# Block-sparse attention and a gated feed-forward: the values' product in column halves, and a hand-set order of all steps

## The chip, the cores and the metric

The kernel runs on one core of a Trainium2 chip. The metric is the device time of one execution in microseconds, as a median over runs. The engines are TensorE (PE; its weight loads are listed apart as PEld), VectorE (DVE), ScalarE (ACT), GpSimd (POOL) and SyncE (SP), which issues most of the DMAs. TensorE writes its results into PSUM; DVE and ACT read them there.

## What is computed

Four batches of eight heads, 768 tokens, 64 columns a head. A token is in one of 24 blocks of 32. A query block sees its neighbours, the first and the last block, and three blocks drawn per query block; the first and the last query block see everything. The attention's result, 512 columns a token, goes through a gated feed-forward layer.

```python
scores = scale * np.matmul(q, k.transpose(0, 1, 3, 2))
...
scores = np.where(mask, scores, -1000000000.0)
scores = scores - np.max(scores, axis=-1, keepdims=True)
attn = np.exp(scores)
attn = attn / (np.sum(attn, axis=-1, keepdims=True) + 1e-09)
return np.matmul(attn, v).astype(np.float32)
...
x = np.ascontiguousarray(attn_out.transpose(0, 2, 1, 3)).reshape(B * S, H * D)
g = x @ w_gate
silu = g * (1.0 / (1.0 + np.exp(-g)))
val = x @ w_val
return (silu * val @ w_out).astype(np.float32)
```

## The kernel before

**Tiles and chunks.** The queries of a batch are 6 tiles of 128 (four blocks each). `CHUNKS` (L29) groups the tiles: batch 0 in three chunks of two, batches 1 to 3 in two chunks of three each, so chunks 3 to 8 hold batches 1 to 3. A chunk goes through attention (`attention`, L1051), then through the feed-forward layer (`ffn_in`, L1611, and `ffn_out`, L1736). Batches 1 to 3 have 22 sparse query blocks each (66 in all): 12 in the first chunk, 10 in the second, whose last tile holds two sparse blocks and the two that see everything.

**Numbers in two parts.** In batches 1 to 3 and in the feed-forward of chunks 2 to 8, a float32 number is held as two float16 numbers, a high part and a low part that is the rest. A product of two such numbers is three float16 products: high by high, high by low, low by high.

**A sparse block of batches 1 to 3** (`block`, L1098). Its keys are copied together into one of three slots (`kring`, by DVE, L1112 to L1115), its values into one of three slots (`vring`: the neighbours by a DMA of SP, L1121, the drawn blocks by an indirect DMA of POOL, L1124). In the order of the steps:
- `scores` (L1131): 32 matmuls (two blocks, eight heads, two parts of the queries) make one step of PE; each uses 32 of the array's columns (four at a time, `tile_position`), into PSUM tile `qk`.
- `top` (DVE, L1151), `power` (ACT, L1168), `inv` (DVE), `high` (ACT, L391) and `low` (DVE, L394): mask and maximum, exponential and sum, reciprocal, weights in two parts into `pp`.
- `turn` (L1193): a DMA transpose on SP's queue into `pts`, of which there are three.
- `product` (L1195): weights times values on PE into PSUM tile `pv`, which two blocks share. For each pair of heads j, over two halves cc of the 256 keys, and over three combinations of parts, one matmul has both heads' values as stationary weights (128 columns) and both heads' attention weights as moving columns (64). The result has 128 rows and 64 columns; only the two quarters in which the head of the values is the head of the weights are used.
- `x_high` (ACT, L1227) and `x_low` (DVE, L1232), once for two blocks: the used quarters go as high and low part into the chunk's input `xall` of the feed-forward, in two operations of 64 partitions each.

The blocks that see everything (`full_rows`, L886) have their own steps. There the scores (L922) and the product (L991) already use 64 columns of the array a matmul, and the product already has the weights' high and low parts side by side: a matmul with the values' high part moves 128 columns, one with the low part 64, and `gather` (L1005) adds the two halves.

**Feed-forward.** For each of 12 groups of 128 hidden columns, `ffn_in` multiplies twice (12 matmuls each, L1693; L1687 in chunks 0 and 1), then ACT and DVE form the gated product, which ACT (`high`, L1712) and POOL (`low`, L1715) split into `h`. `ffn_out` multiplies by the second weight in steps of 9 matmuls (L1756) and stores.

**What sets the order.** All steps are tasks of `Plan` (L120). A task has an engine, a cost in us written beside it, the tasks that it needs, buffers that it takes from rings, and a rank. `order` (L164) plays the program through with these costs: whenever an engine is free, the ready task with the lowest rank (then the earliest number) goes next, if its buffers are free; a task that needs another is ready 0.16 us (`SEM_US`) after the other's end. The order found is the order of the instructions on each engine, and it is fixed when the program is built. Ranks come from the loops (attention of chunk ci at 10 ci, its feed-forward 1000 higher) and a table `SHIFT` (L47) with one number for each key, which several tasks share (a block's whole sequence, for one).

Of the kernel before, what the change touches and what calls it, by code (L numbers as in the profile page):

```python
# [13 lines left out]
ALU = mybir.AluOpType  # L14
# [4 lines left out]
BLK = 32  # L19
# [22 lines left out]
DMA_US = 1.6  # L42
SEM_US = 0.16
# [3 lines left out]
SHIFT = {  # L47
# [54 lines left out]
}  # L102


class Task:
# [122 lines left out]
def tile_block_sparse_attn_swiglu(  # L228
# [1580 lines left out]
    for t in plan.order():  # L1809
        t.emit()  # L1810
# [44 lines left out]
```

## Time and profile before

| | us |
|---|---|
| median of 3 runs | 801.23 (798.42, 801.23, 802.46) |
| profiled execution | 800.0 |
| its span, first to last instruction | 798.2 |
| PE busy | 762.4 |
| DVE busy | 547.4 |
| ACT busy | 504.5 |
| POOL busy | 205.7 |
| mean granted TensorE clock | 0.989 of full speed |

The span is what the profile covers; the execution's time has 1.8 us around it. Busy times count an engine's own instructions, not its waits or the issue of DMAs. PE's matmuls overlap each other, so a matmul's duration (0.19 us for one of 64 columns) is much longer than the step from one start to the next; what a piece of work costs PE is read from its first start to the start of the piece behind it. In a timeline, adjacent instructions of one line are merged and their number stands behind an x.

### The profile page before, as it was taken

Reading aid. Unit: us, or ns where it says so; the run is one execution under the profiler, and the core shown is the slowest. Engines: PE = TensorE matmul, PEld = TensorE weight load, DVE = VectorE, ACT = ScalarE, POOL = GpSimd, SP = SyncE. Lnnn points to the kernel's source line nnn. Section 1 sums busy time; section 2 is a strip of 40 time slices with the busy share of each in tenths; the row PEclk is TensorE's granted clock in tenths of the full one; section 3 lists DMA queues with packets and bytes.
Section 4 is the critical chain, followed back from the end, with each engine's and each line's share of the span. In section 5 each row is a group of like instructions: output and inputs, shape, how many; then the busy total and the mean of one; then the engine's idle time right before and its main releaser. Section 6 shows DMA issues by size and latency. Waiting matters only on the chain.

```text
span 798.2 us, 21196 instructions
## 1 busy us (share of the span) xinstructions
PE 762.4 (96%) x8098; PEld 489.2 (61%) x8098; DVE 547.4 (69%) x1658; ACT 504.5 (63%) x1211; POOL 205.7 (26%) x257
## 2 busy tenths in 40 slices
PE   3789999999999999999999999999999999999998
PEld 2557778884587566645665566645665566555655
DVE  5676898998898787742799866753798767731220
ACT  2687767587688686763598856754487757641221
POOL 3553511322033223201223222401223233101210
PEclk9889999999999999999999999999999999999999
DMA  8963537647877979478769994947878974330001
GB/s 205 259 220 118 193 146 260 205 125 230 198 151 172 212 169 197 91 197 265 159 134 182 269 227 114 203 97 211 188 133 179 228 177 105 69 69 19 1 1 39
DMA packets 171430, 128.08 MB, mean 160 GB/s; under 512 B 115008, under 2 KB 136896, under 8 KB 171328
## 3 DMA queue, kind: packets, MB, share of 16 engines
q1 hardware_dynamic: 165696, 109.42, 56.6%
q0 software_dynamic: 5632, 17.31, 8.5%
q8 instruction: 63, 1.03, 0.5%
q14 instruction: 39, 0.32, 0.1%
HBM read 79.50 MB, written 11.01 MB: 113 GB/s over the span
## 4 chain that ended last, share of the span: by engine, by line
PE 63%; DVE 18%; DMA 8%; issue 4%; ACT 4%; SPq 1%; DVEq 1%; ACTq 0%
PE p L1693 29%; PE po L1756 18%; PE pv L1206 4%; PE p L1687 3%; DMA q<-in_q_dram 3%; PE qk L1137 3%; DVE pp L394 2%; DVE act L1702 1%; DVE act L1707 1%; DMA pts<-pp 1%; DVE w1t L394 1%; DVE e L1151 1%; DMA stage<-in_k_dram 1%; DVE kring L1114 1%; PE qk L1341 1%
## 5 line engine op out<-in xcount | busy, mean ns | idle before, releaser
L1693 PE MATMUL p<-xall,w1t 128*128 128x384 f16 (+1 forms) x2016 | 326.8, 319 | 0.0
L1693 PEld LDWEIGHTS <-w1t 128*128 128x128 f16 x2016 | 191.2, 98 | 115.5 <-issue 8.5
L1715 POOL TENSOR_TENSOR h<-act,h 128x384 f16<-128x384 f32 (+1 forms) x108 | 101.6, 941 | 372.5 <-ACT h L1712 372.1
L1756 PE MATMUL po<-w2all,h 128*128 128x512 f16 (+1 forms) x900 | 195.3, 371 | 0.3 <-DVE w2all L394 0.3
L1756 PEld LDWEIGHTS <-h 128*128 128x128 f16 x900 | 84.6, 98 | 93.7 <-issue 5.6
L1712 ACT CAST h<-act 128x384 f16<-128x384 f32 (+1 forms) x108 | 50.8, 471 | 82.5 <-DVE act L1707 82.2
L1124 POOL DMA_INDIRECT w2all<-vd,vidx x66 | 62.8, 951 | 150.2 <-PE pv L1206 126.7
L1702 DVE SCALAR_TENSOR_TENSOR act<-act,p 128x384 f32<-128x384 f32 (+1 forms) x108 | 54.2, 504 | 65.2 <-ACT act L1698 64.5
L1687 PE MATMUL p<-xall,w1t 128*128 128x256 f32 x384 | 88.8, 384 | 0.4 <-DVE act L1702 0.3
L1168 ACT ACTIVATE e<-e,nb,es 128x256 f32<-128x256 f32 x132 | 78.2, 593 | 2.2
L1687 PEld LDWEIGHTS p<-xall,w1t 128*128 128x128 f32 x384 | 71.4, 192 | 12.0 <-DVE w2all L394 1.4
L1698 ACT ACTIVATE act<-p,gsc 128x384 f32<-128x384 f32 (+1 forms) x84 | 47.0, 560 | 31.2 <-PE p L1693 30.6
L1707 DVE SCALAR_TENSOR_TENSOR act<-act,hs,p 128x384 f32<-128x384 f32 (+1 forms) x84 | 49.7, 591 | 21.8 <-PE p L1693 18.8
L1206 PEld LDWEIGHTS <-w2all 128*128 128x128 f16 x1584 | 55.1, 98 | 13.9 <-issue 3.8
L394 DVE SCALAR_TENSOR_TENSOR pp<-e,rr,pp 128x256 f16<-128x256 f32 x132 | 61.2, 510 | 1.3 <-ACT pp L391 1.0
L391 ACT ACTIVATE pp<-e,rr 128x256 f16<-128x256 f32 x132 | 58.1, 496 | 3.7 <-DVE rr L782 2.5
L1206 PE MATMUL pv<-pts,w2all 128*128 128x64 f16 x1584 | 57.0, 193 | 2.8 <-DMA pts<-pp 2.8
L1151 DVE CUSTOM_DVE_ANT_1 e<-qk,msk 128x256 f32<-128x256 f32 x132 | 50.0, 417 | 2.8 <-issue 2.4
L1593 ACT ACTIVATE ot<-po,oc 128x512 f32<-128x512 f32 (+1 forms) x25 | 16.7, 667 | 42.9 <-PE po L1756 42.7
L1114 DVE COPY kring<-kst 128x256 f16 x198 | 38.9, 251 | 5.6 <-PE qk L1137 5.3
L1232 DVE TENSOR_TENSOR xall<-pv,xall 64x256 f16<-64x256 f32 x66 | 27.7, 420 | 21.1 <-ACT xall L1227 18.7
L1137 PE MATMUL qk<-kring,qs 128*32 128x256 f16 x1056 | 35.7, 274 | 0.2 <-DVE mx L1151 0.2
(187 smaller groups left out, 899.4 us busy)
## 6 DMA issues: line engine op xcount, KB each, us to landing
stage<-in_w_dram SPq DMA_DIRECT2D x36, 512.0 KB
w2all<-vd SPq DMA_DIRECT2D x66, 192.0 KB
qs<-qraw SPq DMA_DIRECT2D x72, 128.0 KB
out_dram<-ot SPq DMA_DIRECT2D x19, 256.0 KB
qn<-in_q_dram SPq DMA_DIRECT2D x36, 128.0 KB
qraw<-in_q_dram SPq DMA_DIRECT2D x36, 128.0 KB
stage<-in_v_dram SPq DMA_DIRECT2D x9, 512.0 KB
vd<-stage SPq DMA_DIRECT2D x9, 512.0 KB
```

The lines of the kernel that those rows point to most:

```text
L391: nc.scalar.activation(hi, src, AF.Copy, scale=scale)
L394: nc.vector.scalar_tensor_tensor(lo, src, scale, hi, op0=ALU.mult, op1=ALU.subtract)
L1124: nc.gpsimd.indirect_dma_start(vf[0:96, 1, :], None, bt.vd, bass.IndirectOffsetOnAxis(ap=vidx[0:96, qb : qb + 1], axis=0))
L1137: nc.tensor.matmul(stv[u * BLK : (u + 1) * BLK, g].rearrange("p s k -> p (s k)"), o.q[:, l, h // 2, h % 2, col : col + BLK], kg[:, h].rear ...
L1151: nc.vector.tensor_tensor_reduce(ev[:, g], stv[:, g], o.g.msk[:, qb, :].unsqueeze(2).broadcast_to([P, 8, BLK]), scale=1.0, scalar=-3.0e38, ...
L1168: nc.scalar.activation(ev[:, g], ev[:, g], AF.Exp, bias=nb_[:, g : g + 1], scale=o.g.es[:, 0:1], accum_out=c["rs"][:, g : g + 1],)
L1206: nc.tensor.matmul(pvv[:, j, n % 2], vg[:, cc, l, 2 * j : 2 * j + 2, :], pq[:, g, m, cc, u : u + 2, :], start=i == 0, stop=i == 5,)
L1687: nc.tensor.matmul(t[:, 0:tc_], w[:, i + 1, k_ * P : (k_ + 1) * P], x_k(k_), start=k_ == 0, stop=k_ == NKT - 1)
L1693: nc.tensor.matmul(t[:, 0:tc_], w_[:, f, m, k_, :], x_k(k_, l), start=i == 0, stop=i == 11)
L1702: nc.vector.scalar_tensor_tensor(a_, a_, 1.0, pg.tile[:, 0:tc_], op0=ALU.add, op1=ALU.mult)
L1715: nc.gpsimd.tensor_tensor(hv(f)[:, 1, :], act.tile[:, 0:tc_], hv(f)[:, 0, :], op=ALU.subtract)
L1756: nc.tensor.matmul(po.tile[:, cs], hv(f)[:, l, ts_], w2h[:, f, m, cs], start=f == 0 and i == 0, stop=f == NF - 1 and i == 2)
```

## The change

Four things, in one diff.

1. `product` of sparse blocks in batches 1 to 3 gives each head its own matmul with 64 stationary columns, in the lower or upper half of the array's columns (`hh`), as `full_rows` has it. The weights' high and low parts lie side by side as moving columns: 64 with the values' high part, 32 (the high part alone) with the low part. 32 matmuls a block in place of 24. `pv` keeps its shape; all of it is used now, as two halves that have to be added.
2. `x_high` copies the first half, rounded to float16, for all 128 partitions at once. `x_low` subtracts that from the first half and then adds the second half.
3. The planner knows column-tiled steps (`thin`): scores and products of batches 1 to 3. Going into or out of a column-tiled stretch costs 0.097 us in its model (`TURN_US`). In such a stretch, a ready column-tiled step goes before any other. A product with `thin=2`, which all have but those of a chunk's last tile, may start outside such a stretch only 4 us (`HOLD_US`) after it is ready. Between two steps of PE the model has no 0.16 us any more. Some costs are changed.
4. `SHIFT` is gone; every task gets a rank of its own from a list, `RANKS`, in the order in which the tasks are made.

```diff
+TURN_US = 0.097
+HOLD_US = 4
...
-SHIFT = {
...
-}
+RANKS = [
+    2700.7, 4581.1, 52.9, 1659, 2895.2, 1629.7, 100.2, 120.7, 2159.2, 8107.9, 4611.5, 731.4, 5241.2, 5293.2, 1337.4,
...
+]
...
-        t.rank = rank + SHIFT.get(t.key, 0.0)
+        t.rank = rank
...
-                    if t.ready > now:
-                        later.append(t.ready)
+                    at = t.ready + (HOLD_US if t.thin == 2 and not thin else 0.0)
+                    if at > now:
+                        later.append(at)
                         continue
-                    if best is not None and (t.rank, t.no) > (best.rank, best.no):
+                    key = (eng == "PE" and thin and not t.thin, t.rank, t.no)
+                    if best is not None and key > low:
                         continue
...
+                us = t.us
+                if eng == "PE":
+                    us += TURN_US if bool(t.thin) != thin else 0.0
+                    thin = bool(t.thin)
...
-                    x.ready = max(x.ready, t.end + SEM_US if x in t.outs else free[eng])
+                    x.ready = max(x.ready, free[eng] if x not in t.outs or eng == x.eng == "PE" else t.end + SEM_US)
...
-            s = in_turn("qk", "PE", 0.87, scores, [o.done] + bt.k_done, rank, take=qk, use=[o.qs, bt.ks])
+            s = in_turn("qk", "PE", 0.66, scores, [o.done] + bt.k_done, rank, take=qk, use=[o.qs, bt.ks], thin=True)
...
-            pvs.append(in_turn("pv", "PE", 0.68, product, there + vl, rank, take=[] if j else [pv],
-                               use=turned + vbuf + ([pv] if j else [])))
+            pvs.append(in_turn("pv", "PE", 0.54, product, there + vl, rank, take=[] if j else [pv],
+                               use=turned + vbuf + ([pv] if j else []), thin=True))
...
-                a = in_turn("qk", "PE", 1.0, lambda first=first: [x[1]() for x in first], [x[0] for x in first] + [o.done], r,
-                            take=qks, use=[o.qs])
+                a = in_turn("qk", "PE", 0.87, lambda first=first: [x[1]() for x in first], [x[0] for x in first] + [o.done], r,
+                            take=qks, use=[o.qs], thin=True)
...
-            pvv = pv.tile.rearrange("p (j b q) -> p j b q", j=4, b=2)
+            out_ = pv.tile.rearrange("p (j b lq) -> p j b lq", j=4, b=2)
 
             for j in range(4):
-                g, u = divmod(2 * j, 4)
-                i = 0
                 for cc in range(2):
-                    for l, m in ((0, 0), (0, 1), (1, 0)):
-                        nc.tensor.matmul(
-                            pvv[:, j, n % 2],
-                            vg[:, cc, l, 2 * j : 2 * j + 2, :],
-                            pq[:, g, m, cc, u : u + 2, :],
-                            start=i == 0,
-                            stop=i == 5,
-                        )
-                        i += 1
+                    for l, w in ((0, 2), (1, 1)):
+                        for hh in range(2):
+                            g, u = divmod(2 * j + hh, 4)
+                            nc.tensor.matmul(
+                                out_[hh * D : (hh + 1) * D, j, n % 2, 0 : w * BLK],
+                                vg[:, cc, l, 2 * j + hh, :],
+                                pq[:, g, 0:w, cc, u, :],
+                                start=cc == 0 and l == 0,
+                                stop=cc == 1 and l == 1,
+                            )
...
         def x_high():
-            for hh in range(2):
-                src, hi, _ = x_views(hh)
-                nc.scalar.copy(hi, src)
+            src, _, hi, _ = x_views()
+            nc.scalar.copy(hi, src)
 
         def x_low():
-            for hh in range(2):
-                src, hi, lo = x_views(hh)
-                nc.vector.tensor_tensor(lo, src, hi, op=ALU.subtract)
+            src, more, hi, lo = x_views()
+            nc.vector.tensor_tensor(lo, src, hi, op=ALU.subtract)
+            nc.vector.tensor_tensor(lo, more, lo, op=ALU.add)
...
-        a = in_turn("pv", "PE", 0.71, product, [a, vl, vi], rank, take=[pv] if n % 2 == 0 else [], use=[pts] + ([pv] if n % 2 else []))
+        a = in_turn("pv", "PE", 0.47, product, [a, vl, vi], rank, take=[pv] if n % 2 == 0 else [], use=[pts] + ([pv] if n % 2 else []), thin=1 if last else 2)
...
-            a = add("ACT", 0.76, x_high, [a, x_open(ci, rank)], rank, use=[pv, xts[ci]])
-            x_done[ci].append(add("DVE", 0.87, x_low, [a], rank, use=[pv, xts[ci]]))
+            a = add("ACT", 0.42, x_high, [a, x_open(ci, rank)], rank, use=[pv, xts[ci]])
+            x_done[ci].append(add("DVE", 0.88, x_low, [a], rank, use=[pv, xts[ci]]))
...
+    for t, rank in zip(plan.tasks, RANKS, strict=True):
+        t.rank = rank
```

The feed-forward's `high` copies also get a dependence on the first copy into the same `h` buffer, in the planner's order alone.

More of the change, by code (lines that the diff above doesn't have):

```diff
@@ L42 @@
 DMA_US = 1.6
+TURN_US = 0.097
+HOLD_US = 4
 SEM_US = 0.16
 LANES = 8
-SHIFT = {
[54 rows of a table removed]
-}
+RANKS = [
[183 rows of a table added]
+]
 class Task:
-    __slots__ = ("eng", "us", "emit", "need", "rank", "take", "dma", "left", "outs", "next", "ready", "end", "no", "key", "late", "many")
+    __slots__ = ("eng", "us", "emit", "need", "rank", "take", "dma", "left", "outs", "next", "ready", "end", "no", "key", "late", "many", "thin")
 class Buf:
@@ L128, in ring, with add @@
         self.depth[name], self.given[name] = n, []
-    def add(self, eng, us, emit, need=(), rank=0.0, take=(), use=(), dma=None, behind=None, late=0.0, many=1):
+    def add(self, eng, us, emit, need=(), rank=0.0, take=(), use=(), dma=None, behind=None, late=0.0, many=1, thin=False):
         t = Task()
+        t.thin = thin
         t.late, t.many = late, many if dma is not None and eng != "POOL" else 0
@@ L174, in order @@
         done = []
+        thin = False
         now = 0.0
@@ L197, in order @@
                         continue
-                    best = t
+                    best, low = t, key
                 if best is None:
@@ L204, in order @@
                     self.given[b.ring].append(b)
-                free[eng] = now + t.us
-                t.end = now + t.us + t.late
+                us = t.us
+                if eng == "PE":
+                    us += TURN_US if bool(t.thin) != thin else 0.0
+                    thin = bool(t.thin)
+                free[eng] = now + us
+                t.end = now + us + t.late
                 if t.dma is not None:
-                    queue = max(max(queue, now + min(0.4, t.us)) + t.dma, t.end)
+                    queue = max(max(queue, now + min(0.4, us)) + t.dma, t.end)
                     t.end = queue + DMA_US
@@ L1087, in attention @@
                 pv = Buf("pv")
-                two = [block(ci, b, bt, o, sub, n + i, sparse[n + i], qbs.index(sparse[n + i]) * BLK, r + 0.05 * i, tsc, pv)
+                two = [block(ci, b, bt, o, sub, n + i, sparse[n + i], qbs.index(sparse[n + i]) * BLK, r + 0.05 * i, tsc, pv,
+                             sub == len(CHUNKS[ci]) - 1)
                        for i in range(2)]
@@ L1096, in attention, with block @@
                         pass
-    def block(ci, b, bt, o, sub, n, qb, col, rank, tsc, pv):
+    def block(ci, b, bt, o, sub, n, qb, col, rank, tsc, pv, last):
         nq = f"{b}_{qb}"
@@ L1215, in block, with x_views @@
         cols = slice(sub * P + col - BLK, sub * P + col + BLK)
-        def x_views(hh):
-            hs_ = slice(hh * D, (hh + 1) * D)
-            pvv = pv.tile.rearrange("p (j b q) -> p j b q", j=4, b=2)
-            src = pvv[hs_, :, :, hh * BLK : (hh + 1) * BLK]
+        def x_views():
+            pvv = pv.tile.rearrange("p (j b l q) -> p j b l q", j=4, b=2, l=2)
             xt = xts[ci].tile
-            return [src] + [xt[hs_, l, :, cols].rearrange("p j (b q) -> p j b q", b=2) for l in range(2)]
+            return [pvv[:, :, :, i, :] for i in range(2)] + [xt[:, l, :, cols].rearrange("p j (b q) -> p j b q", b=2) for l in range(2)]
@@ L1246, in block @@
         a = add("SP", 1.3, turn, [a], rank, take=[pts], use=[pp], dma=1.5)
-        a = in_turn("pv", "PE", 0.71, product, [a, vl, vi], rank, take=[pv] if n % 2 == 0 else [], use=[pts] + ([pv] if n % 2 else []))
+        plan.key = f"c{ci}.{sub}.{n}"
+        a = in_turn("pv", "PE", 0.47, product, [a, vl, vi], rank, take=[pv] if n % 2 == 0 else [], use=[pts] + ([pv] if n % 2 else []), thin=1 if last else 2)
+        plan.key = f"b{ci}.{sub}.{n}"
         v_read[slot] = [a]
         if n % 2 == 1:
-            a = add("ACT", 0.76, x_high, [a, x_open(ci, rank)], rank, use=[pv, xts[ci]])
-            x_done[ci].append(add("DVE", 0.87, x_low, [a], rank, use=[pv, xts[ci]]))
+            a = add("ACT", 0.42, x_high, [a, x_open(ci, rank)], rank, use=[pv, xts[ci]])
+            x_done[ci].append(add("DVE", 0.88, x_low, [a], rank, use=[pv, xts[ci]]))
     def open_q0(ci, rank):
@@ L1729, in ffn_in @@
             new = f % many == 0
-            a = add("ACT", s_[4], high, [a], EVAC, take=[hb] if new else [], use=[act] + ([] if new else [hb]))
+            a = add("ACT", s_[4], high, [a], EVAC, take=[hb] if new else [], use=[act] + ([] if new else [hb]),
+                    behind=None if new else first_h)
+            first_h = a if new else first_h
             h_done.append(add("POOL", s_[5], low, [a], EVAC, use=[act, hb]))
```

236 rows, old and new, of tables (RANKS, SHIFT) are left out of this document.

## The prediction

> **What bounds the kernel now.** I read the page's busy times first, then the chain that ended last, then the busy time by stage, then TensorE's own timeline.
>
> ```profile
> span 798.2 us, 21196 instructions
> PE 762.4 (96%) x8098; PEld 489.2 (61%) x8098; DVE 547.4 (69%) x1658; ACT 504.5 (63%) x1211; POOL 205.7 (26%) x257
> ...
> PE 63%; DVE 18%; DMA 8%; issue 4%; ACT 4%; SPq 1%; DVEq 1%; ACTq 0%
> ```
>
> TensorE (PE) is busy nearly throughout, and the chain runs mostly over it. The stages say where:
>
> ```profile
> 0.00:50.00 50.00, 29.88 (x656) 21.30 (x660) 32.15 (x97) 27.85 (x72) 21.67 (x46) 0.86 0.92 241
> 50.00:150.00 100.00, 95.35 (x1348) 76.03 (x1331) 84.04 (x184) 70.33 (x178) 33.32 (x51) 0.98 0.54 181
> 150.00:725.00 575.00, 567.18 (x5685) 349.91 (x5684) 417.18 (x1354) 390.30 (x935) 139.70 (x149) 1.00 0.73 168
> 725.00:798.20 73.20, 70.00 (x431) 41.95 (x429) 14.04 (x24) 16.01 (x29) 10.96 (x12) 1.00 0.05 15
> ```
>
> The columns are the stretch and its length, then PE, PEld, DVE, ACT and POOL busy with their instruction counts, the granted clock, DMA share and GB/s. From 150 us on PE stands idle 7.8 us before 725 and 3.2 us after, at full clock. So in the stage where the change works, PE time taken away is time gained, as long as PE is still fed. Batch 0 and its loads (first 150 us) hold the other 24.8 us of idle; the new product does not touch them.
>
> How far PE stays fed is read from the end. The chain's last long pieces, and the last attention result:
>
> ```profile
> 724.80 46.80 PE p L1693 x288
> 771.60 23.41 PE po L1756 x144
> ```
>
> ```profile
> L1232 DVE TENSOR_TENSOR xall<-pv,xall x66: 404/422/428, 237.9 to 713.7; 64x256 f16<-64x256 f32 x66
> ```
>
> The last chunk's feed-forward takes 46.80 + 23.41 = 70.2 us, and 3.2 us follow it. It needs all of that chunk's attention, which is finished at 713.7 + 0.4 = 714.1. PE comes to it at 724.8, so attention has 10.7 us in hand.
>
> **The product, piece by piece.** Now each sparse block has 24 matmuls with whole-array weights and 64 moving columns, of which half the output (one head's weights against the other head's values) is thrown away. The columns below are start, duration, engine and what ran:
>
> ```profile
> 308.92 0.86 PE L1206 MATMUL pv<-pts,w2all 128*128 128x64 f16 x24
> 309.62 2.11 PE L1693 MATMUL p<-xall,w1t 128*128 128x384 f16 x12
> 311.57 0.86 PE L1206 MATMUL pv<-pts,w2all 128*128 128x64 f16 x24
> ...
> 314.22 0.86 PE L1206 MATMUL pv<-pts,w2all 128*128 128x64 f16 x24
> ...
> 317.74 4.07 PE L1693 MATMUL p<-xall,w1t 128*128 128x384 f16 x24
> 321.74 0.71 PE L991 MATMUL pvf<-ptsf,stage 128*64 128x128 f16 x24
> 322.38 2.12 PE L1693 MATMUL p<-xall,w1t 128*128 128x384 f16 x12
> 324.44 0.84 PE L922 MATMUL qkf<-kst,qs 128*64 128x384 f16 x8
> ...
> 329.97 1.06 PE L1137 MATMUL qk<-kring,qs 128*32 128x256 f16 x32
> 330.96 2.12 PE L1693 MATMUL p<-xall,w1t 128*128 128x384 f16 x12
> ```
>
> From 308.92 to 309.62 a product holds PE for 0.70 us: 0.70 / 24 = 29 ns a matmul. The new one has 32 matmuls with 64 weight columns, in 16 pairs whose halves lie in different column halves of the array: 8 pairs with 64 moving columns, 8 with 32. The kernel has such pairs already, in the full rows' product (L991), 12 of them, half with 128 and half with 64 columns:
>
> ```profile
> L991 PE MATMUL pvf<-ptsf,stage 128*64 128x128 f16 x144 | 8.2, 226 | 0.0
> L991 PE MATMUL pvf<-ptsf,stage 128*64 128x64 f16 x144 | 7.6, 193 | 0.0
> L1206 PE MATMUL pv<-pts,w2all 128*128 128x64 f16 x1584 | 57.0, 193 | 2.8 <-DMA pts<-pp 2.8
> ```
>
> That piece lasts 0.71 to the end of its last matmul, which takes 0.19 (the 193 ns row), so its 24 matmuls start within 0.52 us: 11 steps of about 47 ns between 12 pairs, the first step slower. If the halves did not run together, 12 matmuls of 64 columns at 29 ns and 12 of 128 at about twice that would take over 1 us. So the halves do run together, and a pair costs about what one whole-array matmul of the same width costs. For the 64-wide pair I take 29 ns. For the 32-wide pair no row has a price; halving gives 15 ns, the 29 ns row is the other end if a step has a floor. I take 29, the nearest row. Then a product is 16 x 0.029 = 0.47 us (0.35 with 15 ns), and 66 blocks (1584 / 24) save 66 x 0.23 = **15.4 us** (23.1 at the other end).
>
> **The turns.** Before a whole-array product an FFN group of 12 takes 311.57 - 309.62 = 1.95. Before a column-tiled piece it takes 324.44 - 322.38 = 2.06, so entering costs 0.10. Leaving: the scores (L1137) hold PE for 330.96 - 329.97 = 0.99. They are 8 steps of four tiles, 256 columns each; at the whole-array rate (1.95 / 12 for 384 columns, so 0.108 for 256) that is 0.87, so 0.12 goes on the first step and on leaving. A group of column-tiled pieces costs **0.22 us** on top of its work. Today the products pay none of it, and the other column-tiled pieces stand alone:
>
> ```profile
> L1137 PE MATMUL qk<-kring,qs 128*32 128x256 f16 x1056 | 35.7, 274 | 0.2 <-DVE mx L1151 0.2
> L922 PE MATMUL qkf<-kst,qs 128*64 128x384 f16 x96 | 10.3, 332 | 0.5 <-ACT ef L944 0.3
> ```
>
> 1056 / 32 = 33 pieces of scores, 96 / 8 = 12 of full-row scores and 288 / 24 = 12 full-row products make 57 groups. The planner now lets a product of a chunk's first tiles wait up to 4 us for company (48 of the 66; the last tiles' 18, which are 4 and 2 in each of three batches, don't wait), and in a column-tiled stretch it picks such pieces first. Products come 2.65 us apart above (308.92, 311.57, 314.22), so a wait of 4 us catches the next one as a rule. My estimate is that the 66 products add 28 groups to the 57, after counting those where scores or full rows share one. Bounds: a few fewer than 57 when nearly every product rides with scores, and 57 + 66 when none does. 28 x 0.22 = **6.2 us lost**.
>
> A group that mixes 32-column scores with 64-column products turns inside as well, if a change of width is a turn; no row has the two side by side. I take nothing for it, and up to 0.22 for each in the range. [...]
>
> **Emptying the products.**
>
> ```profile
> L1232 DVE TENSOR_TENSOR xall<-pv,xall 64x256 f16<-64x256 f32 x66 | 27.7, 420 | 21.1 <-ACT xall L1227 18.7 <-ACT h L1712 1.2 <-issue 0.5
> L1227 ACT CAST xall<-pv 64x256 f16<-64x256 f32 x66 | 24.0, 363 | 18.1 <-PE pv L1206 17.5
> L1469 DVE TENSOR_TENSOR xall<-pv,xall 128x256 f16<-128x256 f32 x3 | 1.2, 414 | 0.0
> L1468 ACT CAST xall<-pv 128x256 f16<-128x256 f32 x3 | 1.1, 370 | 0.0
> ```
>
> ACT does one copy over 128 partitions (0.37) in place of two over 64 (0.73): 33 x 0.36 = 11.9 us of ACT time less, all of it beside PE. DVE still does two operations, at 0.41 in place of 0.42, one of them now an addition of the second half. Neither is on the path; nothing goes into the sum. Its cover is the 10.7 us in hand; were that gone, ACT's part would be a gain.
>
> **A rank per step.** All steps get a new place, on every queue, SP's loads and transposes and POOL's gathers included; PE's steps that follow PE's are modelled without a semaphore's delay. None of that adds an instruction. What it can win is bounded by the idle time: 7.8 us in 150 to 725 and 24.8 before, much of the latter first loads. One stall of the kind that an order can remove:
>
> ```profile
> 350.22 0.16 PE L388 MATMUL nrm_v<-vacc,ones_h 128*128 128x3 bf16 x1 [1.28 <-ACT stage L398]
> ```
>
> I take **3 us gained**, between 8 lost (the idle of 150 to 725 doubled) and 8 gained. The wait added to the products has this queued behind it, off PE:
>
> ```profile
> POOL w2all L1124 <- PE pv L1206: 126.7, 51, 22.1
> ```
>
> The gather of the next values waits for a product to free one of three slots, as the transposes on SP wait for one of three transposed weights. A held product passes its delay on to both. I price that at nothing while the 10.7 us last.
>
> **The sum**: -15.4 + 6.2 - 3 = -12.2 us on the profiled execution's 800.0, so 787.8. The median of the runs shown, 801.2, lies 1.2 above it; on that scale the forecast is **789 us**.
>
> **The rivals.** *Attention sets the end* (17%): if attention still ends at 714.1, the rest is 70.2 + 3.2, a span of 787.5, or 789.3 with the 1.8 around it (800.0 against 798.2) and 790.5 on the median's scale. For it: the slots of three and the single end point; against it: ACT is relieved and the order is free to bring attention forward.
>
> *More than forecast* (13%): 32-wide pairs at 15 ns save 23.1, with 4 us of turns, 3 of idle gained and an earlier end of attention: 801.2 - 22 = 779. It needs attention about 11 us earlier, which speaks against it.
>
> *The change does not group* (13%): the waits seldom find company, 66 new groups cost 14.5 against 15.4 saved, and nothing else is gained: 800. For it are the 18 products that don't wait and stretches in which a product finds no other piece within its wait; against it is the 2.65 us spacing.
>
> *Weight loads set the pace* (5%), slower than before: 16 pairs now bring 16 double loads in 0.47 us, and the densest such stretch seen is this:
>
> ```profile
> 321.74 0.58 PEld L991 LDWEIGHTS <-stage 128*64 128x64 f16 x24 [0.32 <-issue]
> ```
>
> Its 12 pairs of loads, each about 0.11 long, start within 0.47 us, 43 ns a pair. [...] If 43 ns is the loads' own pace, a product takes 16 x 0.043 = 0.69, nothing is saved, and the turns stay: 801.2 + 6.2 = 807. It decides from 44 ns a pair on, where the saving is gone. [...]
>
> *The holds starve PE* (7%), slower too: 8 held products in a chunk go through three slots, 2.7 rounds, at up to 4 us each 10.7 us in a chunk, 21 in the last batch's two. Attention then ends at 735 and the time is 801.2 - 10.7 + 21 = 812. It decides where the holds' delay in the last batch passes 10.7 us.
>
> **How the numbers follow.** My forecast's own case has 45%. A difference of 0.5%, 4 us, is about what a measurement of this kernel can tell from none. Faster than 797 are the forecast, attention's end and the larger gain: 0.75. Within 0.5% is the change that does not group: 0.13. The two slow rivals make 0.12. The range goes from the larger gain, 778, to just over the ungrouped case, 802, and leaves the slow rivals and the best edge out.
>
> **What would show it.** Right: products of 0.46 to 0.49 us from start to start inside a group, pair steps of 28 to 30 ns, 75 to 95 column-tiled groups after 200 us, ACT's busy time down by about 12 us, PE idle in the middle stage still below 10 us, and the last attention result near 705 to 712. Wrong: pair steps over 40 ns (weight loads), 110 groups or more (no grouping), or new PE gaps that end on DMA of the transposes or on gathers, with the last feed-forward starting as soon as the last attention result is there (attention or holds).

## The result, and the profile after

The changed kernel takes 808.6 us (median of 7 runs, 805.4 to 810.3) against 801.1 for the kernel before (7 runs, 798.4 to 810.2): a ratio of **1.0081, 95% interval 1.0052 to 1.0111**. 789 was forecast, with 802 as the upper end. Here and below, a ratio leaves out runs more than 1.5% above the fastest run of their kernel, which are one of before's and four of the twelve of e11_pairs_slot. The profiled execution took 810.32 us, its span is 808.5.

Busy times of the changed kernel:

```profile
span 808.5 us, 22153 instructions
PE 761.2 (94%) x8626; PEld 484.3 (60%) x8626; DVE 548.1 (68%) x1658; ACT 491.5 (61%) x1178; POOL 206.6 (26%) x257
```

PE did not become less busy (762.4 before), though the product is less work, and the span grew by 10.3. By stage, columns as in the prediction:

```profile
50.00:150.00 100.00, 95.47 (x1398) 77.33 (x1397) 86.97 (x191) 74.11 (x188) 37.31 (x53) 0.97 0.57 192
150.00:725.00 575.00, 556.11 (x6165) 339.25 (x6164) 415.27 (x1346) 375.19 (x899) 138.31 (x148) 0.99 0.77 168
725.00:808.50 83.50, 79.86 (x478) 46.57 (x476) 15.86 (x33) 17.91 (x31) 10.94 (x12) 1.00 0.05 17
```

Between 150 and 725 us PE stands idle 18.9 us (7.8 before), and the granted clock, 1.00 before, is 0.99. Both are losses inside the stage that was to gain. The last attention results and the last chunk's feed-forward:

```profile
L1368 DVE TENSOR_TENSOR xall<-pv,xall x33: 423/424/425, 238.5 to 725.1; 128x256 f16<-128x256 f32 x33
```

```profile
734.50 46.96 PE L1831 MATMUL p<-xall,w1t 128*128 128x384 f16 x288
```

Attention ends at 725.5, 11 us later than before, and PE comes to the last feed-forward at 734.5, 10 us later. Attention still has 9 us in hand: it does not set the end. PE lost its time on the way. PE's waits in the changed kernel (engine, line, what was waited for: total, times, longest; the four longest of batches 1 to 3 and the feed-forward):

```profile
PE p L1831 <- ACT xall L1363: 3.3, 2, 1.7
PE pv L1346 <- DMA pts<-pp: 3.0, 4, 1.3
PE pv L1346 <- issue: 2.2, 6, 0.5
PE qk L1277 <- issue: 2.1, 5, 0.7
```

In the kernel before, the longest row of these stages is this one; its hand-overs from attention to the feed-forward show no wait:

```profile
PE pv L1206 <- DMA pts<-pp: 2.8, 3, 1.3
```

Three things are new against before. The first is waits for operands that used to be there. Both waits of the first row are like this stretch of PE's timeline (start, duration, engine, what ran, idle time ahead of it):

```profile
459.67 0.81 PE L1896 MATMUL po<-w2all,h 128*128 128x512 f16 x3
460.41 0.68 PE L1346 MATMUL pv<-pts,w2all 128*64 128x64 f16 x32
461.92 0.68 PE L1346 MATMUL pv<-pts,w2all 128*64 128x64 f16 x32 [0.82 <-DMA pts<-pp]
464.25 0.32 PE L1831 MATMUL p<-xall,w1t 128*128 128x384 f16 x1 [1.65 <-ACT xall L1363]
465.18 3.49 PE L1831 MATMUL p<-xall,w1t 128*128 128x384 f16 x11 [0.61 <-DVE xall L1368]
```

The new order puts a chunk's feed-forward right behind that chunk's last product. PE has to sit through the copy on ACT and two operations on DVE that turn the product into the feed-forward's input; nothing else stands in its queue at this place.

The second is in the last row: 11 matmuls of 384 columns take 3.49 us, 0.32 each, twice the 0.16 that they have elsewhere. The stages around three such places show why (stretches of 5 us; the granted clock is the third number from the end):

```profile
465.00:470.00 5.00, 4.82 (x20) 2.46 (x20) 1.85 (x6) 2.88 (x7) 0.00 (x0) 0.66 1.21 219
250.00:255.00 5.00, 4.25 (x26) 3.27 (x26) 4.90 (x22) 3.77 (x12) 1.56 (x2) 0.66 1.00 245
555.00:560.00 5.00, 3.54 (x14) 1.79 (x14) 0.85 (x2) 4.53 (x7) 0.92 (x1) 0.76 1.00 271
256.00:261.00 5.00, 5.00 (x96) 4.22 (x95) 4.82 (x23) 3.92 (x13) 2.45 (x3) 1.00 0.79 179
```

At these three places, 2.3 to 3.1 us of idle time close together are followed by half the clock for about 3.4 us, then it is back (the last row is 6 us behind the second). Here the stop cost its own time and up to 1.7 us on top (half of the 3.4), and PE looked busy meanwhile.

Such stops are not always followed by half clock. In e2_order_only (below), which has the same order, PE stops for 2.9 us at the hand-over shown above, and goes on at 0.16 us a matmul:

```profile
462.79 0.32 PE L1835 MATMUL p<-xall,w1t 128*128 128x384 f16 x1 [2.30 <-ACT e L1308]
463.68 1.95 PE L1835 MATMUL p<-xall,w1t 128*128 128x384 f16 x11 [0.57 <-DVE xall L1372]
```

Of 37 stops of 2.2 to 3.1 us after 200 us in the traces of all the runs (idle times less than 2.5 us apart added up), 20 were followed by half clock. So the size of the stops alone does not set how much half clock an execution shows.

The third is "issue": stops that no semaphore ends, inside long groups of column-tiled pieces:

```profile
431.03 1.78 PE L1346 MATMUL pv<-pts,w2all 128*64 128x64 f16 x84
433.34 0.39 PE L1346 MATMUL pv<-pts,w2all 128*64 128x64 f16 x12 [0.53 <-issue]
433.66 1.02 PE L1277 MATMUL qk<-kring,qs 128*32 128x256 f16 x22
435.36 0.53 PE L1277 MATMUL qk<-kring,qs 128*32 128x256 f16 x10 [0.69 <-issue]
```

**The whole account.** From TensorE's matmul starts I worked out, from 200 us to the end, how long each piece held PE until the next one's start, and took off its steady time (dense matmuls 163 ns at 384 columns, 109 at 256, 216 at 512; old product 0.70; new one 16 pairs of 32 ns, 0.507; scores 0.872). What is left is sorted by what ended it. The columns are the kernels before and after and five of the experiments below (P: the new product in the order of before; PP: the same with products side by side; O: the old product in the new order; O-: that without holds; A-: the changed kernel without holds). Each column is one profiled execution, in us, and they come from several chips:

| | before | after | P | PP | O | O- | A- |
|---|---|---|---|---|---|---|---|
| column-tiled groups | 57 | 59 | 121 | 100 | 50 | 50 | 79 |
| 66 products' steady time | 46.2 | 33.5 | 33.5 | 33.5 | 46.2 | 46.2 | 33.5 |
| turns and slow first steps | 13.1 | 20.2 | 26.1 | 23.4 | 15.1 | 12.4 | 20.7 |
| waits for operands | 5.1 | 13.8 | 7.2 | 15.3 | 16.1 | 14.0 | 14.1 |
| visible issue stops | 0.1 | 4.4 | 0 | 0.3 | 0.3 | 0 | 0 |
| half clock | 0 | 4.8 | 1.6 | 0 | 2.0 | 1.9 | 1.1 |
| sum | 64.5 | 76.7 | 68.4 | 72.5 | 79.7 | 74.5 | 69.4 |

After against before: 12.7 us of work saved; 7.1 more at turns, of which about 5.1 are what pieces take above the median of their kind (I take them for stops too short to be listed, which isn't shown), so 2.0 are turns proper; 8.7 more waits; 4.3 visible issue stops; 4.8 at half clock. That is 12.2 us lost. (The dense work left at 200 us is 2.4 less than in before, hence 9.8 at the end. In O and O- it is 6.3 and 6.9 less, so that their spans are only 8.5 and 3.6 longer, with sums 15.2 and 10.0 higher.)

### The profile page after: what moved, and what is told of

The parts are those of the page before. It is cut to its first block, busy times and chain, and to the rows that moved or that the text cites. A ratio compares the mean times of both kernels' runs of the same rounds, so it can differ in the third digit from the quotient of the medians.

```text
span 808.5 us, 22153 instructions
## 1 busy us (share of the span) xinstructions
PE 761.2 (94%) x8626; PEld 484.3 (60%) x8626; DVE 548.1 (68%) x1658; ACT 491.5 (61%) x1178; POOL 206.6 (26%) x257
## 4 chain that ended last, share of the span: by engine, by line
PE 65%; DVE 16%; DMA 8%; issue 4%; ACT 4%; SPq 2%; DVEq 0%; POOL 0%; ACTq 0%
PE p L1831 33%; PE po L1896 17%; PE pv L1346 4%; PE qk L1277 4%; DMA q<-in_q_dram 3%; PE p L1825 2%; DMA stage<-in_k_dram 1%; PE qk L1479 1%; DVE act L1845 1%; DVE w1t L571 1%; DVE pp L533 1%; DVE w1t L572 1%; PE pvf L1130 1%; DMA qn<-in_q_dram 1%; DVE act L1840 1%
## 5 line engine op out<-in xcount | busy, mean ns | idle before, releaser
L1831 PEld LDWEIGHTS <-w1t 128*128 128x128 f16 x2016 | 196.1, 99 | 124.3 <-issue 12.7
L1853 POOL TENSOR_TENSOR h<-act,h 128x384 f16<-128x384 f32 (+1 forms) x108 | 98.0, 908 | 386.3 <-ACT h L1850 381.3
L1896 PE MATMUL po<-w2all,h 128*128 128x512 f16 (+1 forms) x900 | 192.7, 371 | 0.6 <-DVE w2all L533 0.6
L533 DVE SCALAR_TENSOR_TENSOR pp<-e,rr,pp 128x256 f16<-128x256 f32 x132 | 63.7, 524 | 7.8 <-ACT pp L530 5.6
L1845 DVE SCALAR_TENSOR_TENSOR act<-act,hs,p 128x384 f32<-128x384 f32 (+1 forms) x84 | 49.4, 590 | 23.4 <-PE p L1831 22.0
L1346 PEld LDWEIGHTS <-w2all 128*64 128x64 f16 x2112 | 38.6, 113 | 17.5 <-issue 16.6
L1346 PE MATMUL pv<-pts,w2all 128*64 128x64 f16 (+1 forms) x2112 | 42.8, 190 | 5.4 <-DMA pts<-pp 3.0
L1305 ACT ACTIVATE nb<-mx,es 128x2 f32<-128x2 f32 x66 | 19.1, 289 | 27.6 <-DVE mx L1291 22.4
```

Source lines behind the costliest of these rows:

```text
L533: nc.vector.scalar_tensor_tensor(lo, src, scale, hi, op0=ALU.mult, op1=ALU.subtract)
L1346: nc.tensor.matmul(out_[hh * D : (hh + 1) * D, j, n % 2, 0 : w * BLK], vg[:, cc, l, 2 * j + hh, :], pq[:, g, 0:w, cc, u, :], start=cc == 0 ...
L1831: nc.tensor.matmul(t[:, 0:tc_], w_[:, f, m, k_, :], x_k(k_, l), start=i == 0, stop=i == 11)
L1845: nc.vector.scalar_tensor_tensor(a_, a_, sc, pw.tile[:, 0:tc_], op0=ALU.mult, op1=ALU.mult)
L1853: nc.gpsimd.tensor_tensor(hv(f)[:, 1, :], act.tile[:, 0:tc_], hv(f)[:, 0, :], op=ALU.subtract)
L1896: nc.tensor.matmul(po.tile[:, cs], hv(f)[:, l, ts_], w2h[:, f, m, cs], start=f == 0 and i == 0, stop=f == NF - 1 and i == 2)
```

## The experiments

Ratios are to runs of the kernel before on the same chip, with the 95% interval. The theories that the expectations speak of: **A**, the product saves what the pieces show, and the new order loses it in waits; **B**, the product itself costs; **C**, holding products back starves the attention behind them, through SP's queue (**C1**) or the three transposed buffers (**C2**); **D**, runs of small instructions outrun their supply; **O**, the order as a whole leaves attention's pieces no slack.

**Product and order apart.** e1_product_only puts the new product and its copies into the kernel before; e2_order_only puts the old product and copies into the changed kernel. (The cuts of code in this part are shortened and carry remarks.)

```diff
-for l, m in ((0, 0), (0, 1), (1, 0)):   # e1, in the kernel before; e2 the reverse, in the changed one
+for l, w in ((0, 2), (1, 1)):
+    for hh in range(2):
```

> The new product, its two copies and nothing else: the order of all steps is that of the kernel before, to the instruction. Theory A (the product saves what its pieces show, the new order loses it again in waits of PE): a product that stands alone takes 0.45 of work and 0.27 of turns, 0.72 against 0.70, so 66 of them are 1 us slower; 799 to 804. Theory B (the product itself is what costs, by its weight loads or its 32 matmuls): most of the 8 us is here already, 806 to 810. PE waits behind column-tiled pieces stay under 3 us by A.

> The new order of all steps to the instruction, with the old product (24 whole-array matmuls) and the old copies in it. Theory A: slower than the changed kernel or like it, 808 to 820, since the waits stay and 66 products are some 0.17 us longer each, partly inside the waits. Theory B: without the new product the loss goes, 795 to 802.

e1: **1.0036 (1.0010 to 1.0063)**. e2: **1.0102 (1.0055 to 1.0149)**. The order alone costs as much as the whole change; the new product alone is nearly neutral. One of e1's products between two feed-forward groups:

```profile
311.45 2.12 PE L1689 MATMUL p<-xall,w1t 128*128 128x384 f16 x12
313.50 0.68 PE L1206 MATMUL pv<-pts,w2all 128*64 128x64 f16 x32
314.11 2.12 PE L1689 MATMUL p<-xall,w1t 128*128 128x384 f16 x12
```

It holds PE for 0.61 and makes the group ahead of it 0.10 longer (2.05 from start to start instead of 1.95): 0.71 together, against 0.70 for the old one. The rest of e1's 0.36% is a little more waiting and half clock (column P). So theory A is right in where the loss sits, though its other half, that the product saves much by itself, fails: alone it saves nothing, since each pays its turns.

**Company in the order of before.** e3_pairs is e1 with 22 pairs of products side by side: where a feed-forward step stood between two products, it goes ahead of the first.

```diff
+for t, f, u in zip(pe, pe[1:], pe[2:]):   # product, feed-forward step, product
+    done.remove(f); done.insert(at[id(t)], f)
```

> As the first of these runs (order of before, new product), but wherever PE had product, one feed-forward step, product, that feed-forward step is put ahead of the first product: 22 pairs side by side, no group longer than two products, the other engines' order untouched. Theory A: a pair takes 1.22 with its turns in place of 2 x 0.72, so 22 x 0.2 = 4 to 5 us less than the first run, 795 to 799, PE waits as in before. Theory B: no gain over the first run. Theory C (holding products back starves the three slots): slower than the first run by 2 us or more.

**1.0119 (1.0079 to 1.0160)**: 0.8% worse than e1, where pairs should have saved 0.5%. The turns did fall, by 2.7 us (26.1 to 23.4), and the waits rose by 8.1 (7.2 to 15.3). They are of one kind. PE's longest wait outside its first loads, in e1 and then in e3:

```profile
PE nrm_v L388 <- ACT stage L398: 4.4, 2, 2.8
```

```profile
PE pv L1238 <- DMA pts<-pp: 10.9, 9, 2.0
```

A first product that is about 2 us later makes later products' transposed weights late. Theory C has the right sign here.

**Prices by themselves.** e4_bench is the kernel before with runs of matmuls on data already on the chip added at its end.

```diff
+whole(256); halves(128); whole(64); thin32(64)
+8 x (quarters(4); few(16)); 8 x (whole_b(32); few(16)); whole(64)
```

> The kernel before with a run of matmuls on PE put behind it, whose results nobody reads: 256 whole-array ones with 64 columns, then 128 times a pair of 64 and a pair of 32 columns in column halves (the new product's pattern without any data to wait for), 64 pairs of 32 columns, then eight times 16 matmuls in column quarters and 32 in column halves in turn, then whole-array and column halves in turn. Theory A: the pattern of the product keeps its 56 ns for two pairs. Theory D (the instruction supply can't keep up with 4 instructions in 28 ns): the pattern starts at 56 ns and then stops for some 0.5 us every 256 instructions or so, a mean of 60 to 90 ns for two pairs, while the whole-array run has no such stops. A change from quarters to halves costs 0.2 us as a turn does, or nothing.

Whole-array matmuls, then the product's pattern of 64- and 32-wide pairs (256 pairs), and further on a 64-column piece between two 32-column ones:

```profile
798.81 7.63 PE L233 MATMUL bench<-w2all 128*128 128x64 f16 x256
806.37 2.62 PE L243 MATMUL bench<-w2all 128*64 128x64 f16 x153
810.06 2.21 PE L243 MATMUL bench<-w2all 128*64 128x64 f16 x128 [1.07 <-issue]
813.81 2.21 PE L243 MATMUL bench<-w2all 128*64 128x64 f16 x128 [1.53 <-issue]
817.28 1.79 PE L243 MATMUL bench<-w2all 128*64 128x64 f16 x103 [1.26 <-issue]
...
828.73 0.62 PE L258 MATMUL bench<-w2all 128*32 128x256 f16 x16
829.28 0.69 PE L253 MATMUL bench<-w2all 128*64 128x64 f16 x32
829.91 0.62 PE L258 MATMUL bench<-w2all 128*32 128x256 f16 x16
```

Column pairs start 32 ns apart, whether 64 or 32 columns wide: 128 matmuls of the mixed pattern in 2.21 us, whose last takes 0.19, are 63.5 steps of a pair in 2.02 us; of 32-wide ones alone, 89 matmuls take 1.60, the last of them 0.18, 44 steps in 1.42. (Start to start it is 3 to 4 ns from one half of a pair to the other and 28 to 29 to the next pair.) But PE stops after every 128 matmuls, which with their weight loads are 256 instructions; from one stop's end to the next 128 matmuls take 3.5 to 3.75 us, 27 to 29 ns each instead of 16. The first 256 whole-array matmuls, at 30 ns each, have no stop. For two pairs that is 109 to 117 ns, more than the 60 to 90 that theory D expected, and the stops are two to three times its 0.5 us. The row for the instruction queue on this run's page has the same unit. Its 78 packets in 1.28 MB are 16.4 KB each, and the 10018 matmuls of the run (8098 and the bench's 1920) with as many loads are 78.3 times 256 instructions; in the kernel before it is 63 packets for 16196, 257 each.

```profile
q8 instruction: 78, 1.28, 0.6%
```

So the stops that theory D expected are there in this bench: PE ran whole-array matmuls at 30 ns for 256 in a row, and column-tiled ones, at 16 ns, for 128 at a time. That the supply of instructions is what stops it is my reading of the common unit of 256. A change of width costs like a change to whole-array and back (0.22 in the prediction): 0.55 + 0.63 us for the two pieces, against 0.44 + 0.51 without turns (4 steps of 109 ns, 16 of 32), so 0.23 for both changes.

**The values' loads moved from SP to POOL**, to take them out of the transposes' queue (C1): e5_pairs_pool, e6_after_pool, e7_before_pool, e8_product_pool are e3, the changed kernel, the kernel before and e1 with this.

```diff
-nc.sync.dma_start(...)      # neighbours' values, L1121
+nc.gpsimd.dma_start(...)
```

> The run with 22 hand-made pairs, but the loads of a sparse block's neighbour values are issued by POOL, next to its gather of the drawn values, and no longer by SP. In the pairs run SP waited 43 us for products at these loads (28 in before), with the transposes of later blocks behind them on the same queue, and PE waited 11 us for those transposes. Theory C1 (SP's queue passes a held product on to the transposes behind it): PE's waits for transposes fall below 4 us, and the time to 796 to 803. Theory C2 (the three transposed buffers pass it on, or the transposes are simply later): no change, 807 to 812.

> The changed kernel with the same move of the value loads from SP to POOL, all else as it is. Theory C1: its waits for transposes, masks and keys shrink; 800 to 805 against its 808.6. Theory C2: 806 to 811.

> The kernel before with the same move, as a control: by C1 and C2 alike 797 to 803, since its waits for transposes are 2.8 us in all; slower if POOL's own cost for issuing the loads counts.

> The new product in the order of before (no pairs) with the same move: the control for the pairs. By the sum of pieces the pairs run with the move is 4 to 5 us faster than this one (22 x 0.2); if pairing in itself costs (instruction supply, later values), it isn't.

e5 1.0301 (1.0256 to 1.0345), e6 1.0046 (1.0020 to 1.0073), e7 1.0144 (1.0114 to 1.0175), e8 1.0173 (1.0143 to 1.0204). The move by itself costs the kernel before 1.4%, as its waits go from 5.1 to 19.1 us, so it is no clean test. Paired products stay worse than single ones (e5 against e8), so SP's queue was not their only trouble. That the changed kernel gains by the move (1.0081 to 1.0046) isn't clear of noise, as the intervals overlap. Its waits rise from 13.8 to 20.3 us, against what C1 expected. But its issue stops are gone, with PE's order as it was: the group that stopped twice at 431 us in the changed kernel runs through here, all 128 matmuls.

```profile
427.04 1.70 PE L1346 MATMUL pv<-pts,w2all 128*64 128x64 f16 x96
428.67 1.06 PE L1277 MATMUL qk<-kring,qs 128*32 128x256 f16 x32
```

So the length of a group alone does not decide whether it stops; what else does isn't shown.

**Holds undone.** In e9_split a product that follows a feed-forward step and has other column-tiled pieces behind it goes ahead of that step, where by the order's own times its operands were there (11 products). In e14_as_ready every product goes ahead of all steps that it had been held past (21 products); e18_order_ready is e2 with the same edit. e10_dense_first does the contrary: the feed-forward step behind each of 53 groups goes ahead of it.

```diff
+if there <= f.ready:            # operands there when the step f starts
+    done.remove(t); done.insert(at[id(f)], t)      # e9, e14, e18
+done.remove(f); done.insert(at[id(group[0])], f)   # e10
```

> The changed kernel with its order mended in one respect: a product that stands behind a feed-forward step and ahead of other column-tiled pieces goes ahead of that step, where by the kernel's own plan its operands were there already (11 products; 59 column-tiled groups become 70). Theory C (holding a product back for company starves the attention behind it): 11 more groups cost 11 x 0.27 = 3.0 us, but the stops behind thin groups, about 21 us more than in the kernel before, shrink by more than that: 800 to 806. Theory O (the order as a whole leaves no slack, the 11 holds are a small part of it): the groups' cost shows and little is won, 808 to 812. Theory D (long runs of small instructions outrun their supply): the stops that no semaphore ends, 4.4 us after 200 us, fall below 2.

> The changed kernel with each column-tiled group and the feed-forward step behind it changed over (53 of 59 groups), so that every piece of attention comes about 2 us later to TensorE against its operands, with the groups as they are. Theory O (pieces come to TensorE just when, or before, their operands land; the order has no slack): TensorE's waits for attention's operands (about 12 us) go down to 6 or less and the time falls to 800 to 804. Theory C (each delay of a piece is handed on through three slots to the next ones): what each piece gains is lost by the next, waits stay or grow, 808 to 818.

> The changed kernel with every held product put back: 21 products go ahead of the feed-forward steps that the planner let pass while the product's operands were there already (59 column-tiled groups become 79). Theory C (holding costs more than the company saves; e9_split won 4.4 us net with 11 of them at 11 more groups): 20 more groups cost 5.4 us and the time still falls, to 800 to 805, no higher than e9_split. Theory C' (only the 11 that hold other pieces up matter; the rest are free in this order): the other ten add their turns and win nothing, so 1 to 3 us above e9_split, 806 to 809.

> The old product and copies in the changed kernel's order with the 21 held products put back (e2_order_only with the edit of e14_as_ready). If the holds are all that is wrong with the order (theory C), the ratio falls from e2_order_only's 1.010 to 1.000 to 1.004. If the order has no slack apart from the holds (theory O), it stays at 1.006 to 1.012, and the new product's 16 us less of work are what brings e14_as_ready down to 1.0059.

e9: **1.0026 (1.0001 to 1.0050)**; e14: **1.0059 (1.0036 to 1.0082)**; e18: **1.0117 (1.0091 to 1.0143)**; e10: **1.0255 (1.0218 to 1.0293)**. Undoing holds helps the changed kernel, more turns and all: in e9 by 0.5%, just outside the noise, in e14 by 0.2%, within it. Whether e14's ten further products cost anything isn't clear either, as the intervals of e9 and e14 overlap. In the account, two entries of e14 are lower. Its issue stops are gone (4.4 to 0; in e9 they are 2.3, where D expected less than 2), and no group of it has more than three pieces. Its half clock falls too (4.8 to 1.1), which need not be the holds' doing: it still has stops of 2.4 us at 248 and 2.8 us at 460, and half clock did not follow them. Its waits for operands are as before (14.1 against 13.8), and e18 shows that they belong to neither the holds nor the product: with the old product and no holds the order still costs 1.2% and waits 14.0 us. PE's waits in e18 from 200 us on, the longest of them, the hand-over of a chunk among them as in the changed kernel:

```profile
PE pv L1371 <- DMA pts<-pp: 3.6, 4, 1.6
...
PE p L1860 <- ACT xall L1392: 3.2, 2, 2.3
PE p L1860 <- DVE act L1869: 2.4, 1, 2.4
...
PE qk L1302 <- DVE mx L1316: 1.9, 2, 1.6
```

With the old product, which isn't column-tiled, undoing the holds wins nothing (1.0102 and 1.0117), perhaps because there are no long column-tiled runs to break up. Theory C as the whole cause falls; theory O keeps the larger share. But O's own remedy in e10, to give every piece about 2 us more, failed badly, as C had expected: waits rose to 25.5 us, and the transposes lead them.

```profile
PE pv L1374 <- DMA pts<-pp: 11.7, 10, 2.5
```

My reading, which no run tests further: a delayed piece delays the attention that needs its slot or its result, so a later place for all pieces is as bad as holding some. What the order lacks is slack between each piece's operands and its place, and pushing pieces back did not add it.

**A fourth buffer for transposed weights** (C2; smaller scratch rings, and a small table laid into the space of `xall`, make room): e11_pairs_slot, e12_after_slot, e13_split_slot, e15_ready_slot, e16_before_slot and e17_product_slot are e3, the changed kernel, e9, e14, the kernel before and e1 with this.

```diff
-buf.tile = pool.tile(shape, dt, tag=buf.ring, name=name, bufs=n)
+buf.tile = pool.tile(shape, dt, tag=buf.ring, name=name, bufs=n + (buf.ring == "pts"))
-def small_t(shape, tag, name, bufs=6, dt=F32):
+def small_t(shape, tag, name, bufs=4, dt=F32):
```

> The kernel with the new product in the order of before and 22 pairs of products side by side, with a fourth buffer for the transposed weights (small scratch tiles in four instead of six buffers make room). Theory C2 (a late product keeps one of three transposed buffers, and the next transposes wait for it): the 11 us of waits for transposes in that kernel go below 5 and the ratio to the kernel before falls from 1.012 to 1.000 to 1.004. If the transposes are late for another reason (the issuing queue, or the exponentials): ratio 1.010 to 1.014.

> The changed kernel with a fourth buffer for the transposed weights (small scratch tiles in four instead of six buffers make room). Only 3 us of its TensorE waits end on the transposes, so theory O (an order with no slack at many operands) expects 805 to 809; theory C2 expects the waits on transposes gone and what follows from them too, 800 to 805.

> The best of the changed orders so far, e9_split (1.0026), with the fourth buffer for the transposed weights. If what is left of its loss is still delay handed on through the buffers, 0.995 to 1.000; if it is the turns and the order at large, within 0.2% of e9_split, 1.001 to 1.005.

> The kernel of e14_as_ready with a fourth buffer for the transposed weights as well. If the three buffers still pass delays on once nothing is held, it falls another 2 to 4 us, to 797 to 802, level with the kernel before or under it; if the buffers only mattered for held products, it is within 2 us of e14_as_ready.

> The kernel before with a fourth buffer for the transposed weights, a control for the kernels that have it. Its waits on transposes are 2.8 us in all, so at most that can be won: ratio 0.996 to 1.001. If it is below 0.995, the buffer helps by itself and the gain of e11_pairs_slot over e3_pairs says less about held products.

> The new product in the order of before, ungrouped, with a fourth buffer, beside e11_pairs_slot (1.0026), which differs only in its 22 pairs. The pairs save 22 x 0.22 = 4.8 us of turns: if the fourth buffer takes all of what holding costs, this kernel is 0.4 to 0.6% above e11_pairs_slot, 1.006 to 1.009; if the hold's cost is still there in part, the two are level or this one is below, 0.999 to 1.003.

e11 1.0026 (0.9985 to 1.0066), e12 1.0071 (1.0041 to 1.0101), e13 1.0024 (1.0006 to 1.0043), e15 1.0035 (1.0004 to 1.0065), e16 1.0014 (0.9986 to 1.0042), e17 1.0025 (0.9999 to 1.0050). The buffer does nothing measurable for the kernel before, the changed kernel, e1, e9 or e14. The paired products come down from 1.0119 to 1.0026, the time that C2 expected. But that is the ratio of eight of twelve runs: all twelve lie between 798.6 and 813.7 us with a median of 808.5, 1.0075 times the 802.5 of the kernel before beside them. And the waits that were to vanish are there still:

```profile
L1238 PE MATMUL pv<-pts,w2all 128*64 128x64 f16 (+1 forms) x2112 | 41.9, 190 | 11.6 <-DMA pts<-pp 11.6
```

So whether the buffer helps the pairs isn't shown, nor by what, and C2 stays open. Even at 1.0026 the pairs are only level with single products (e17), and no version is faster than the kernel before.

## Why the prediction was wrong, point by point

**What bounds the kernel**: right. PE's queue sets the end before and after.

**The product**: the way right, the size too good. Inside a group a product takes 0.507 us from start to start, not 0.47, since a pair's step is 32 ns: the 29 that I took is the step of single whole-array matmuls, and a pair adds the 3 to 4 ns between its halves. That a 32-wide pair costs as much as a 64-wide one, the end that I took, is right. 66 blocks save 12.7 us and not 15.4 (66 x 0.23 is 15.2). "Weight loads set the pace" did not come true, as 32 ns is below its 44; what sets the 32 isn't shown.

**The turns**: mis-sized, and the make-up wrong. 2.0 us of turns proper, 6.2 forecast. 59 groups, not 85, so the planner found more company than I gave it. From the medians of the changed kernel's pieces, entering costs 0.10, and 0.02 more if a product comes first; leaving costs 0.118 behind scores and 0.087 behind a product; one product behind another costs nothing, scores behind a product 0.083 and a product behind scores 0.115. So a product next to another saves 0.20, about what I took, but next to scores only the 0.10 of entering. "A change of width: I take nothing" was wrong: it costs what leaving costs.

**Emptying**: right. ACT is busy 13.0 us less (11.9 forecast); the time shows no gain from it.

**"A rank per step: I take 3 us gained"**: this step failed. The order alone costs 1.0 to 1.2% (e2, e18), 8 to 9 us, the far end of the 8 lost that I allowed. I had expected a gain because an order can remove idle time, and looked at no row that shows how long before its piece each operand lands. With 5.1 us of waits after 200 us the order of before had that slack, and the new one doesn't: 13.8 to 16.1 us in all four kernels with it in the account.

**"A held product passes its delay on to both. I price that at nothing while the 10.7 us last"**: this failed too, as the rule by which it was priced is wrong. 9.0 us are in hand at the end of the changed kernel as well, and 10.9 in e3_pairs, whose held products still cost 0.8%. Time in hand at the end pays for a delay only if PE has something else to run meanwhile; its queue has a fixed order, and whatever stands behind a late piece stands still. The rival "the holds starve PE", with its 10.7 us as the point of decision, has the same fault. That its 812 comes near the result is luck: by it, attention would have ended at 735 and set the end, and it ended at 725.5 with 9.0 us in hand.

**Not foreseen**: issue stops in long column-tiled groups, 4.3 us visible and perhaps 5.1 in short steps, and 4.8 us at half clock. With 8.7 us of waits they make 22.9, more than the 10.7 that work and turns gain (12.7 less 2.0).

**"The change does not group"** (800): e1 is this case, and came out at 1.0036, about 804, though the change did group. The saving and the turns nearly cancel there, as its price has it (12.7 against 13.0 us); 3.7 us of waits and half clock come on top.

What stays open: why the new order waits more, and what decides whether a long group stops. The ranks, the missing delay between PE's steps and the preference for column-tiled pieces were made together, and only the holds were taken out alone.

## What to carry to other kernels

Price a new order of an in-order engine by the slack of each piece (operand landed to piece started), not by idle time now nor by time in hand at the end: a late piece stops all that is queued behind it (here PE waited 13.8 to 16.1 us, 5.1 before, with 9.0 in hand at the end). Column tiling that nearly halves the time of a matmul nearly doubles the rate of instructions (16 ns against 30 here); check in a trace that a whole group runs through at that rate before making groups longer (in e4_bench PE stopped after every 128 such matmuls). Take the step of a pair from the start of one pair to the start of the next, both halves included. A stop of 2 to 3 us on TensorE can cost 1.7 us more for half clock behind it; in these traces about half of them did.

## What the runs showed of the hardware

- At 16 ns a matmul (column pairs at 32 ns) PE in e4_bench stopped for 1.1 to 1.5 us after every 128 matmuls with 128 loads; in 256 matmuls at 30 ns it did not. Whole-array matmuls that came behind column-tiled ones stopped too, for 0.84, 0.22 and 0.26 us.
- A 32-wide pair takes 32 ns in e4_bench, as a 64-wide one does: halving the moving columns gained nothing.
- The clock in the first 150 us, where the new product doesn't run, differs between profiled executions: by the granted clock in stretches of 5 us, 8.5 us' worth is missing there in the kernel before, 11.9 in the changed one, 15.4 in e14, 5.1 in e13. Single executions that differ by a few us are to be read with that in mind; the account above starts at 200 us for this reason.
